# Mamba-2 scan with a quick-GELU layer on one core: second group's first two blocks by seven block products, w_in's sums in four portions, four buffers for x

## The chip, the core and the metric

The kernel runs on one core of a Trainium2 chip. A core has a matrix engine (TensorE, "PE" in the profile, with its weight loads as "PEld"), a vector engine (VectorE, "DVE"), a scalar engine (ScalarE, "ACT"), GpSimd ("POOL") and the engine that issues most of the transfers here (SyncE, "SP"). Each works through its own list of instructions in order, and waits on semaphores that other engines and transfers raise. The metric is the device time of one execution in microseconds (us); of several runs the median is given.

## The reference

A chunked state-space scan gives 3072 tokens of 256 channels, and a two-layer network with a quick-GELU follows. Cut to what matters:

```python
# x (4, 8, 768, 32), a (4, 8, 768), B and C (4, 8, 768, 16)
for c in range(nc):                                   # chunks of 32
    cum = np.cumsum(log_a[:, :, sl], axis=-1)
    L = np.exp(cum[:, :, :, None] - cum[:, :, None, :]) * causal
    y[:, :, sl] = einsum('bhij,bhjd->bhid', (Cc @ Bc^T) * L, xc) \
                  + einsum('bhin,bhnd->bhid', Cc, state) * np.exp(cum)[..., None]
    state = decay_full * state + sum_j(Bc_j xc_j decay_from_j)
x = y.transpose(0, 2, 1, 3).reshape(3072, 256)
h = x @ w_in                                          # (256, 2048), float64 weights
out = (h * sigmoid(1.702 * h)) @ w_out                # (2048, 256)
```

The weights come as 64-bit floats, and the kernel makes 32-bit ones of them on VectorE and ScalarE in the first 70 us.

## The kernel before

**Tiling.** The 3072 tokens are six groups (g = 0 to 5) of TG = 512. A group has two "pairs" of 128-token chunks, numbered p or k = 2g and 2g+1. For a group the scan's result is yT[g] (256 channels by 512 tokens, as two halves of channels and two of tokens). The 2048 hidden rows are 16 tiles of 128, taken two at a time as eight blocks j = 0 to 7; gT[g, j] holds a block's activations.

**The scan of a pair.** `decay(p)` is one long VectorE scan (L402, into L) and two small products (`ends`, Be, L461). `gain` makes 56 small matmuls into the banks A (L711); `part_of` masks A into the state S, on ScalarE (L762) or VectorE (L764); `add_up` chains the states (L777); `since_start` makes CsT (L665). `turn_blocks` transposes B and C on VectorE (L635); `mask_blocks` makes CT on ScalarE (L657); `score` makes 64 small matmuls into cb (L680); `weigh` multiplies L by cb on VectorE (L691). `finish` step 0 ("inter") makes y from the old state (L816), step 1 ("intra") from L and x (L828), and ScalarE copies y into yT (L855). cb, y and the sums acc of w_out's products share one area of PSUM, so each waits for the readers of the one before.

**A block as whole products or as seven block products.** `hidden(g, f)` makes one hidden tile by two products of 512 columns (L884) and one ScalarE silu (L888). `first(g, j, i)` makes a block (two hidden tiles) by seven products of 128 by 128 by 256 instead of eight, in the Strassen-Winograd manner. It needs sums of w_in (`mix_in(n)`: four VectorE instructions for blocks 2n and 2n+1) and of yT (`mix_y(g)`, three instructions, L908 to L910). In the lists of steps "j.i" is product i of block j: 1, 6, 7, 4 add up in a bank X, and between them ScalarE copies the partial sum out (L945: after 1 and 7 into ac, after 6 into b), which the next product of X waits for; after 4 it takes the silu of X (L917). 5, 2, 3 go into a bank Y. D is the VectorE sum of Y and ac (L1072, 512 columns), S its silu; after 3 comes the VectorE sum of Y and b (L1072, 256 columns), T is its silu. X, Y and A take turns on four PSUM banks ("ff"), so a new X or Y waits for the last reader of an older one. `product(g, j, i)` are the seven products with w_out ("P", L1045, and L1052 in the last group); they need `mix_w` (sums of w_out, L1005) and `mix_g(g, j)` (sums of gT, L908 to L910).

**Order around the change.** The order on each engine is the order of the code (`in_order` at the end fixes it). Group 0 is done by whole products: 16 `hidden`, then `project_all` (w_out, L982), with the second pair's conversion and scan work hung in between by `at(in_project[0], i, ...)`. Then group 1 begins: blocks 0 and 1 by `hidden(1, f)`, f = 0 to 3, with group 2's scan work after the first two and the output of group 0 (`turn_out`, two VectorE transposes, L1099, and eight output transfers) after the others; then blocks 2 to 7 by seven products:

```python
at(after, "H0", lambda: decay(n + 1), lambda: mix_y(1), lambda: since_start(n),
   lambda: since_start(n + 1), lambda: gain(later), lambda: keep_both(later, True), lambda: score(later),
   lambda: weigh(n), lambda: weigh(n + 1))
at(after, "H1", lambda: turn_out(0, 0), lambda: turn_out(0, 1))
...
run(1, "2.1 3.1 2.5 2.6 3.6 z 2.2 2.7 3.5 3.7 3.2 2.D 2.4 3.D 3.4 2.S W 2.3 3.S 3.3 2.T 3.T y",
    z=lambda: finish(later, (0,)), y=lambda: finish(later, (1,)), W=lambda: mix_w(0))
for j in range(2):
    mix_g(1, j)
run(1, "4.1 4.5 4.2 P P 4.6 P L P 4.7 P P P 4.D", seven(1, 0), L=more_loads)
```

From group 2 on every block is done by seven products, and `mix_in(0)`, for blocks 0 and 1, is made at the end of group 1. Some products in group 1 are issued in two or four parts of the columns (n in `hidden` and in `product`).

**Transfers.** All of SP's transfers are in one list. `load(p)` brings the pair's b and x (and from group 2 on the blocks zC and zB); `spread(p)` brings the decay factors a; each x tile has three buffers, so x of pair 5 takes the buffer of pair 2 and waits for its last reader.

Of the kernel before, what the change touches and what calls it, by code (L numbers as in the profile page):

```python
# [8 lines left out]
FP32 = mybir.dt.float32  # L9
# [7 lines left out]
P = 128  # L17
# [18 lines left out]
def kernel(  # L36
# [31 lines left out]
    nc = tc.nc  # L68
# [69 lines left out]
    def load(p, parts=None):  # L138
# [4 lines left out]
        for part in parts:  # L143
            dst, src, e = {"b": (rb, B, N), "c": (rc, C, N), "x": (rx, x, D)}[part]
            dst[p] = raw.tile([P, 2, NH, e], FP32, tag=part, name=f"{part}{p}",
                              bufs=2 if part == "c" else 3)
            for k in range(2):
                b, c = divmod(2 * p + k, NC)
                sl = slice(c * P, (c + 1) * P)
                nc.sync.dma_start(out=dst[p][:, k], in_=src[b, :, sl, :].rearrange("h s d -> s h d"))  # L150
# [567 lines left out]

    steps = const.tile([P, Q * D, 2 * CG], FP32, name="steps")
    drop = ffn.tile([P, 4, TG // 2], FP32, tag="my", name="drop", bufs=1)[:, :2].rearrange(  # L720
# [171 lines left out]

    def mix_in(n):

# [5 lines left out]
        for o, u, v, op in ((s1, a21, a22, ALU.add), (s2, s1, a11, ALU.subtract),  # L900
                            (s3, a11, a21, ALU.subtract), (s4, a12, s2, ALU.subtract)):
            nc.vector.tensor_tensor(out=o, in0=u, in1=v, op=op)
        for k in range(2):
# [112 lines left out]
    def product(g, j, only=ORDER, ks=range(2)):  # L1016
# [22 lines left out]
        for i in only:  # L1039
            w, h = terms[i]  # L1040
            if g < NG - 1:
                n = 2 if g == 1 and 7 * j + ORDER.index(i) < 0 else 1
                for k in range(n):
# [181 lines left out]
    for i, k, c in ((2, 1, 1), (3, 2, 2), (4, 4, 4), (5, 6, 8), (6, 9, 12), (7, 12, 15)):  # L1225
# [12 lines left out]
       lambda: weigh(PG), lambda: weigh(PG + 1))  # L1238
    at(in_project[0], 13, lambda: finish(pairs, (0,)))
    at(in_project[0], 15, lambda: finish(pairs, (1,)))  # L1240
    at(in_project[0], 13, lambda: mix_in(1), lambda: mix_in(2), lambda: mix_in(3),
       lambda: turn_blocks(2), lambda: decay(n))
    at(in_project[0], 6, lambda: spread(n), lambda: load(n), lambda: load_blocks(n + 1),
# [3 lines left out]

    after = {}

    later = n, n + 1  # L1250
    at(after, "H0", lambda: decay(n + 1), lambda: mix_y(1), lambda: since_start(n),
       lambda: since_start(n + 1), lambda: gain(later), lambda: keep_both(later, True), lambda: score(later),
       lambda: weigh(n), lambda: weigh(n + 1))
    at(after, "H1", lambda: turn_out(0, 0), lambda: turn_out(0, 1))
    assert [b for b in range(NB) if 3 * CG <= b * NC < 4 * CG] == [2]
# [6 lines left out]
    project_all(0, in_project[0])  # L1262
    mask_blocks(n)
    mask_blocks(n + 1)
    load(p)
    spread_rows(2)
    for step in "H0", "H1":
        for i in range(2):
            hidden(1, 2 * int(step[1:]) + i)
        for do in after[step]:  # L1270
            do()

    def run(g, steps, products=(), **do):
# [36 lines left out]
    def more_loads():  # L1310
# [3 lines left out]

    run(1, "2.1 3.1 2.5 2.6 3.6 z 2.2 2.7 3.5 3.7 3.2 2.D 2.4 3.D 3.4 2.S W 2.3 3.S 3.3 2.T 3.T y",
        z=lambda: finish(later, (0,)), y=lambda: finish(later, (1,)), W=lambda: mix_w(0))
    for j in range(2):
        mix_g(1, j)
    run(1, "4.1 4.5 4.2 P P 4.6 P L P 4.7 P P P 4.D", seven(1, 0), L=more_loads)
    mix_w(1)  # L1320
# [10 lines left out]
    mix_g(1, 6)  # L1331
    mix_in(0)
    run(1, "P P A P P P P P", seven(1, 5), A=lambda: ahead(2, p))
    mix_g(1, 7)

    for g in range(2, NG):
# [44 lines left out]
        else:  # L1381
            run(g, "2.1 1.S 1.4 1.3 2.6 2.5 2.2 2.7 1.T 2.D M0 3.1 3.5 2.S 2.4 3.6 2.3 3.2 3.7 2.T 3.D M1",
                M0=lambda: mix_g(g, 0), M1=lambda: mix_g(g, 1))
# [56 lines left out]
```

## Time and profile before

| | us |
|---|---|
| median of 3 runs | 352.09 (350.5 to 352.2) |
| the profiled execution | 350.75 |
| its span, first to last instruction | 348.7 |
| TensorE busy | 342.2 (98%) |
| VectorE busy | 254.4 (73%) |
| ScalarE busy | 151.7 (44%) |

The granted TensorE clock is 1.000. The page's slices show how the engines are filled over the span; each digit is the busy share of 8.7 us in tenths:

```profile
PE   8989999999999999999999999999999999999996
...
DVE  5989998899679998739996548788454654455463
ACT  5598683106454323744342544432554321554320
```

Group 1 begins in the tenth slice (81.65 us). A row of the timeline gives the start, the length, the engine, the line, the operation, the tiles, the shapes and the number of instructions merged in it; in brackets stands how long the engine had been idle and what ended that. One product of 256 columns shows as two matmul records; the records overlap, so a product's pitch is shorter than its two lengths together. "SPq" rows are transfers being issued, not moved.

### The profile page before, as it was taken

The page shows a single profiled execution, that of the slowest core. Times are in us where ns is not written, and L with a number is a line of the kernel's source. Part 1 is how long each engine was busy: PE and PEld are TensorE (multiplying, and loading weights), DVE is VectorE, ACT ScalarE, POOL GpSimd, SP SyncE. Part 2 cuts the span into 40 slices and gives each one's busy share as a digit, 9 for nine tenths or more (in the row PEclk, how much of TensorE's full clock was granted, in tenths as well). Part 3 has the DMA queues.
Part 4 walks back from the last instruction along what each step waited for, and adds up shares of the span by engine and source line. Part 5 has one row for each costly group of instructions (what it writes and reads, how often), then busy time and mean ns, then how long its engine had stood idle before and what let it go on. Part 6 is the DMA issues. An engine that isn't in the chain of part 4 may idle for free.

```text
span 348.7 us, 8126 instructions
## 1 busy us (share of the span) xinstructions
PE 342.2 (98%) x3386; PEld 273.8 (79%) x3386; DVE 254.4 (73%) x476; ACT 151.7 (44%) x348; POOL 13.8 (4%) x42
## 2 busy tenths in 40 slices
PE   8989999999999999999999999999999999999996
PEld 6634444548888888888888888888888888899996
DVE  5989998899679998739996548788454654455463
ACT  5598683106454323744342544432554321554320
POOL 8400000100000100000000000000000000000000
PEclk9999999999999999999999999999999999999999
DMA  6599988453626100445703026400000300000301
GB/s 160 114 352 192 242 180 222 80 92 69 118 46 138 46 0 9 70 88 107 112 22 55 2 75 112 74 0 3 0 4 2 61 2 0 0 2 0 62 0 61
DMA packets 89980, 25.92 MB, mean 74 GB/s; under 512 B 73432, under 2 KB 87128, under 8 KB 89944
## 3 DMA queue, kind: packets, MB, share of 16 engines
q1 hardware_dynamic: 89112, 24.88, 33.5%
q10 hardware_dynamic: 832, 0.52, 0.6%
q8 instruction: 26, 0.43, 0.5%
q14 instruction: 10, 0.08, 0.1%
HBM read 22.15 MB, written 3.24 MB: 73 GB/s over the span
## 4 chain that ended last, share of the span: by engine, by line
PE 95%; DVE 2%; DMA 2%; SPq 0%; ACT 0%; issue 0%; DVEq 0%
PE acc L1045 28%; PE X L940 19%; PE Y L950 14%; PE h L884 9%; PE o L982 8%; PE acc L1052 7%; PE y L828 2%; PE cb L680 2%; DMA bits<-in_moe_w_in_dram 2%; PE y L816 1%; PE A L711 1%; PE busy L440 1%; PE ab L554 1%; SPq L180 0%; DVE c L1076 0%; PE ab L548 0%
## 5 line engine op out<-in xcount | busy, mean ns | idle before, releaser
L945 ACT ACTIVATE ac<-X 128x256 f32<-128x256 f32 x76 | 29.1, 383 | 78.7 <-PE X L940 78.2
L1045 PE MATMUL acc<-mg,mw 128*128 128x256 f32 x192 | 54.5, 379 | 0.0
L917 ACT ACTIVATE gT<-gT 128x512 f32<-128x512 f32 (+1 forms) x76 | 39.3, 520 | 33.5 <-DVE gT L1072 32.8
L1072 DVE TENSOR_TENSOR gT<-Y,ac 128x512 f32<-128x512 f32 x38 | 26.2, 689 | 36.5 <-PE Y L950 29.9
L940 PE MATMUL X<-my,mi 128*128 128x256 f32 x152 | 45.1, 379 | 0.0
L1072 DVE TENSOR_TENSOR gT<-Y,b 128x256 f32<-128x256 f32 x38 | 15.8, 419 | 34.4 <-PE Y L950 34.4
L1045 PEld LDWEIGHTS acc<-mg,mw 128*128 128x128 f32 x192 | 36.5, 190 | 5.0
L884 PE MATMUL h<-yT,w_in 128*128 128x512 f32 (+2 forms) x108 | 35.7, 486 | 1.4 <-DVE w_in L228 1.4
L1045 PE MATMUL acc<-gT,w_out 128*128 128x256 f32 x128 | 35.5, 379 | 0.0
L884 PEld LDWEIGHTS h<-yT,w_in 128*128 128x128 f32 x108 | 18.3, 190 | 17.3 <-issue 14.9
L940 PEld LDWEIGHTS X<-my,mi 128*128 128x128 f32 x152 | 28.0, 190 | 3.7
L982 PE MATMUL o<-gT,w_out 128*128 128x512 f32 x64 | 28.6, 597 | 0.0
L908 DVE TENSOR_TENSOR mg<-gT 128x512 f32<-128x512 f32 x40 | 27.2, 681 | 0.0
L1045 PEld LDWEIGHTS acc<-gT,w_out 128*128 128x128 f32 x128 | 24.2, 190 | 3.4 <-ACT yT L855 0.2
L945 ACT ACTIVATE b<-X 128x256 f32<-128x256 f32 x38 | 14.6, 384 | 20.2 <-PE X L940 19.8
L940 PE MATMUL X<-yT,w_in 128*128 128x256 f32 x76 | 23.2, 389 | 0.0
L950 PE MATMUL Y<-my,mi 128*128 128x256 f32 x76 | 22.7, 381 | 0.1
L950 PE MATMUL Y<-yT,w_in 128*128 128x256 f32 x76 | 22.7, 381 | 0.0
L940 PE MATMUL X<-my,w_in 128*128 128x256 f32 x76 | 22.5, 379 | 0.0
L950 PE MATMUL Y<-yT,mi 128*128 128x256 f32 x76 | 22.5, 379 | 0.0
L982 PEld LDWEIGHTS o<-gT,w_out 128*128 128x128 f32 x64 | 11.8, 190 | 13.2 <-issue 12.7
L402 DVE TENSOR_TENSOR_SCAN L<-a,idents 128x1024 f32<-128x1024 f32 x9 | 20.5, 2277 | 0.1
(152 smaller groups left out, 545.3 us busy)
## 6 DMA issues: line engine op xcount, KB each, us to landing
a<-scratch SPq DMA_DIRECT2D x18, 256.0 KB, 5.4
bits<-in_moe_w_out_dram SPq DMA_DIRECT2D x8, 512.0 KB, 5.8
x<-in_x_dram SPq DMA_DIRECT2D x24, 128.0 KB, 3.1
out_dram<-ob SPq DMA_DIRECT2D x40, 64.0 KB, 1.9
bits<-in_moe_w_in_dram SPq DMA_DIRECT2D x8, 256.0 KB, 5.1
bits<-in_moe_w_in_dram SPq DMA_DIRECT2D x4, 512.0 KB, 9.7
b<-in_B_dram SPq DMA_DIRECT2D x20, 64.0 KB, 2.9
af<-in_a_dram SPq DMA_DIRECT2D x3, 384.0 KB
```

Source lines behind the costliest of these rows:

```text
L402: nc.vector.tensor_tensor_scan(out=L, data0=ra[p].rearrange("p k e -> p (k e)"), data1=idents.rearrange("p h i -> p (h i)"), initial=0.0, ...
L680: nc.tensor.matmul(out=s["cb"][side, r, k].rearrange("p (q i) -> p q i", q=Q), lhsT=BT[rows, k, side], rhs=CT[rows, k, :, side], start=Tru ...
L884: nc.tensor.matmul(out=h[:, cols], lhsT=w_in[:, f, k], rhs=yT[g][:, k, cols], start=(k == 0 and e == 0), stop=(k == NK - 1), skip_group_ch ...
L908: nc.vector.tensor_tensor(out=t[:, 0:2], in0=B[:, :, 1], in1=B[:, 0], op=ALU.subtract)
L917: nc.scalar.activation(o, i, AF.Silu, scale=GELU_SCALE)
L940: nc.tensor.matmul(out=s["X"], lhsT=lhsT, rhs=rhs, start=i == "1", stop=i == "4", skip_group_check=True)
L945: nc.scalar.activation(copy, s["X"], AF.Copy)
L950: nc.tensor.matmul(out=o, lhsT=lhsT, rhs=rhs, start=s.pop("new", False), stop=i != "5", skip_group_check=True)
L982: nc.tensor.matmul(out=o[c], lhsT=w_out[:, c, f], rhs=gT[g, f // 2][:, f % 2], start=(f == 0), stop=(f == NF - 1), skip_group_check=True)
L1045: nc.tensor.matmul(out=acc[g][0][i][:, cols], lhsT=w, rhs=h[:, cols], start=(j == 0 and k == 0 and (i, 0) in begins), stop=(j == NF // 2 - ...
L1052: nc.tensor.matmul(out=o[k] if type(o) is list else o[:, cols], lhsT=h[:, cols], rhs=w, start=(j == 0 and (i, k) in begins), stop=(j == NF ...
L1072: nc.vector.tensor_tensor(out=o, in0=v, in1=w, op=ALU.add)
```

## The change

Six edits. (1) Blocks 0 and 1 of group 1 are made by seven block products each, in the list of steps, instead of by `hidden`; group 2's scan work is placed among them (G: `gain` and VectorE's `part_of`, C: `score`, t: `since_start`, A and B: `add_up`, w: `weigh`); ScalarE's part of `keep_both` for these pairs becomes VectorE's. (2) `mix_in(0)` moves from the end of group 1 to the projection of group 0; `mix_in(1)` to m, after 0.D; `mix_in(2)` and `mix_in(3)` to V and U, before 2.D. (3) `turn_blocks(2)`, `mask_blocks` of both pairs and `decay(n)` move ahead in the projection of group 0. (4) x has four buffers, and `steps` takes a turn of the "ob" tiles. (5) `turn_out(0, ...)` moves behind the first products with w_out (o). (6) The first eight products with w_out in group 1 are issued in halves of their columns, and in the last group 2.4 stands ahead of 3.5. The parameter `engine` of `mix_in` isn't used by any call.

```diff
--- before.py
+++ after.py
@@ -143,7 +143,7 @@
         for part in parts:
             dst, src, e = {"b": (rb, B, N), "c": (rc, C, N), "x": (rx, x, D)}[part]
             dst[p] = raw.tile([P, 2, NH, e], FP32, tag=part, name=f"{part}{p}",
-                              bufs=2 if part == "c" else 3)
+                              bufs={"c": 2, "b": 3, "x": 4}[part])
             for k in range(2):
                 b, c = divmod(2 * p + k, NC)
                 sl = slice(c * P, (c + 1) * P)
@@ -716,7 +716,8 @@
                             skip_group_check=True)
             increment[p] = [t[:, 2 * n:2 * n + 2] for t in A] if pairs[0] else A
 
-    steps = const.tile([P, Q * D, 2 * CG], FP32, name="steps")
+    steps = ffn.tile([P, 2, DM], FP32, tag="ob", name="steps").rearrange(
+        "p k (e m) -> p (k e) m", m=2 * CG)
     drop = ffn.tile([P, 4, TG // 2], FP32, tag="my", name="drop", bufs=1)[:, :2].rearrange(
         "p a (e m) -> p (a e) m", m=2 * CG)
     nc.gpsimd.memset(drop[:, :, 0:1], 0.0)
@@ -890,7 +891,7 @@
 
     mixed_in, mixed_y, chain = {}, {}, {}
 
-    def mix_in(n):
+    def mix_in(n, engine=nc.vector):
 
         t = wide.tile([P, PN], FP32, tag=("m", "p2")[n % 2], name=f"mi{n}").rearrange(
             "p (j s e) -> p j s e", j=2, s=4)
@@ -899,7 +900,7 @@
         s1, s2, s3, s4 = (t[:, :, i] for i in range(4))
         for o, u, v, op in ((s1, a21, a22, ALU.add), (s2, s1, a11, ALU.subtract),
                             (s3, a11, a21, ALU.subtract), (s4, a12, s2, ALU.subtract)):
-            nc.vector.tensor_tensor(out=o, in0=u, in1=v, op=op)
+            engine.tensor_tensor(out=o, in0=u, in1=v, op=op)
         for k in range(2):
             mixed_in[2 * n + k] = t[:, k]
 
@@ -1039,7 +1040,7 @@
         for i in only:
             w, h = terms[i]
             if g < NG - 1:
-                n = 2 if g == 1 and 7 * j + ORDER.index(i) < 0 else 1
+                n = 2 if g == 1 and 7 * j + ORDER.index(i) < 8 else 1
                 for k in range(n):
                     cols = slice(k * HT // n, (k + 1) * HT // n)
                     nc.tensor.matmul(out=acc[g][0][i][:, cols], lhsT=w, rhs=h[:, cols],
@@ -1237,21 +1238,15 @@
     at(in_project[0], 9, lambda: score(pairs), lambda: gain(pairs), lambda: keep_both(pairs, True),
        lambda: weigh(PG), lambda: weigh(PG + 1))
     at(in_project[0], 13, lambda: finish(pairs, (0,)))
+    at(in_project[0], 13, lambda: turn_blocks(2), lambda: mask_blocks(n), lambda: mask_blocks(n + 1))
     at(in_project[0], 15, lambda: finish(pairs, (1,)))
-    at(in_project[0], 13, lambda: mix_in(1), lambda: mix_in(2), lambda: mix_in(3),
-       lambda: turn_blocks(2), lambda: decay(n))
+    at(in_project[0], 13, lambda: decay(n), lambda: mix_in(0))
     at(in_project[0], 6, lambda: spread(n), lambda: load(n), lambda: load_blocks(n + 1),
        lambda: load(n + 1, "b"), lambda: spread(n + 1))
     at(in_project[0], 9, lambda: load(n + 1, "x"))
 
 
-    after = {}
-
     later = n, n + 1
-    at(after, "H0", lambda: decay(n + 1), lambda: mix_y(1), lambda: since_start(n),
-       lambda: since_start(n + 1), lambda: gain(later), lambda: keep_both(later, True), lambda: score(later),
-       lambda: weigh(n), lambda: weigh(n + 1))
-    at(after, "H1", lambda: turn_out(0, 0), lambda: turn_out(0, 1))
     assert [b for b in range(NB) if 3 * CG <= b * NC < 4 * CG] == [2]
 
 
@@ -1260,16 +1255,8 @@
         for do in in_hidden[0].get(f, []):
             do()
     project_all(0, in_project[0])
-    mask_blocks(n)
-    mask_blocks(n + 1)
     load(p)
     spread_rows(2)
-    for step in "H0", "H1":
-        for i in range(2):
-            hidden(1, 2 * int(step[1:]) + i)
-        for do in after[step]:
-            do()
-
     def run(g, steps, products=(), **do):
 
 
@@ -1312,11 +1299,25 @@
         load(p + 1)
         spread(p + 1)
 
-    run(1, "2.1 3.1 2.5 2.6 3.6 z 2.2 2.7 3.5 3.7 3.2 2.D 2.4 3.D 3.4 2.S W 2.3 3.S 3.3 2.T 3.T y",
-        z=lambda: finish(later, (0,)), y=lambda: finish(later, (1,)), W=lambda: mix_w(0))
+    def keep_later():
+        gain(later)
+        for k in later:
+            part_of(k, range(4), False)
+
+    def add_later(i):
+        add_up(later[i], range(4))
+
+    decay(n + 1)
+    mix_y(1)
+    run(1, "0.1 0.2 G 0.5 0.6 C t A 0.7 1.1 1.2 0.D m 0.4 1.6 B 1.5 0.3 0.S 1.7 2.1 0.T 1.D w 1.4",
+        G=keep_later, A=lambda: add_later(0), B=lambda: add_later(1), C=lambda: score(later), t=lambda: [since_start(k) for k in later], m=lambda: mix_in(1), w=lambda: (weigh(n), weigh(n + 1)))
+    run(1, "1.S 3.1 1.3 1.T 2.5 2.6 3.6 2.2 z 2.7 3.5 3.7 3.2 V U 2.D 2.4 3.D 3.4 2.S W 2.3 3.S 3.3 y 2.T 3.T",
+        z=lambda: finish(later, (0,)), y=lambda: finish(later, (1,)), W=lambda: mix_w(0), m=lambda: mix_in(1), V=lambda: mix_in(2), U=lambda: mix_in(3),
+        w=lambda: (weigh(n), weigh(n + 1)))
     for j in range(2):
         mix_g(1, j)
-    run(1, "4.1 4.5 4.2 P P 4.6 P L P 4.7 P P P 4.D", seven(1, 0), L=more_loads)
+    run(1, "4.1 4.5 4.2 P P 4.6 P L P 4.7 P o P P 4.D", seven(1, 0), L=more_loads,
+        o=lambda: (turn_out(0, 0), turn_out(0, 1)), U=lambda: mix_in(3))
     mix_w(1)
     mix_g(1, 2)
     decay(p)
@@ -1329,7 +1330,6 @@
     k = NF // 2 - 1
     run(1, closing(k), seven(1, 4))
     mix_g(1, 6)
-    mix_in(0)
     run(1, "P P A P P P P P", seven(1, 5), A=lambda: ahead(2, p))
     mix_g(1, 7)
 
@@ -1379,7 +1379,7 @@
             if most:
                 decay(p)
         else:
-            run(g, "2.1 1.S 1.4 1.3 2.6 2.5 2.2 2.7 1.T 2.D M0 3.1 3.5 2.S 2.4 3.6 2.3 3.2 3.7 2.T 3.D M1",
+            run(g, "2.1 1.S 1.4 1.3 2.6 2.5 2.2 2.7 1.T 2.D M0 3.1 2.4 2.S 3.5 3.6 2.3 3.2 3.7 2.T 3.D M1",
                 M0=lambda: mix_g(g, 0), M1=lambda: mix_g(g, 1))
         for j in range(5 if more else 4, NF // 2):
             if j == 5:
```

## The prediction

> **What bounds the kernel now.** First the page: TensorE is busy for nearly the whole span, and the chain that ended last is TensorE for 95%.
>
> ```profile
> PE 342.2 (98%) x3386; PEld 273.8 (79%) x3386; DVE 254.4 (73%) x476; ACT 151.7 (44%) x348; POOL 13.8 (4%) x42
> PE 95%; DVE 2%; DMA 2%; SPq 0%; ACT 0%; issue 0%; DVEq 0%
> ```
>
> Then the view of waits for TensorE: it lists no wait behind 22 us. The view of windows for the changed stretch, 81.65 (first hidden product of group 1) to 99.62 (product 4.1), says the same: TensorE 17.97 of 17.97 us, VectorE 14.17.
>
> ```profile
> PE h L884 <- DVE w_in L228: 1.4, 1, 1.4
> 81.65:99.62 17.97, 17.97 (x385) 15.44 (x383) 14.17 (x30) 10.60 (x29) 0.00 (x0) 1.00 0.49 93
> ```
>
> So a gain has to be TensorE work taken away, and what VectorE and ScalarE make late comes back as TensorE waits. The timeline of the stretch has the rows I price with (start us, length us):
>
> ```profile
> 70.70 2.35 DVE L691 TENSOR_TENSOR L<-L,cb 128x1024 f32<-128x1024 f32 x2
> ...
> 77.36 1.09 DVE L635 STREAM_TRANSPOSE Ct<-zC 128x512 f32<-128x512 f32 x1
> ...
> 79.26 2.22 DVE L402 TENSOR_TENSOR_SCAN L<-a,idents 128x1024 f32<-128x1024 f32 x1
> 79.26 1.00 SPq L150 DMA_DIRECT2D x<-in_x_dram  x2
> ...
> 81.65 3.71 PE L884 MATMUL h<-yT,w_in 128*128 128x128 f32 x28
> ...
> 81.92 2.28 DVE L402 TENSOR_TENSOR_SCAN L<-a,idents 128x1024 f32<-128x1024 f32 x1
> ...
> 85.28 0.84 PE L711 MATMUL A<-x,Be 64*32 64x64 f32 x56
> ...
> 86.10 1.20 PE L680 MATMUL cb<-CT,Bt 32*64 32x128 f32 x64
> 86.18 1.70 ACT L762 ACTIVATE S<-A,part 128x64 f32<-128x64 f32 x8 [0.19 <-PE A L711]
> ...
> 87.23 3.72 PE L884 MATMUL h<-yT,w_in 128*128 128x256 f32 x16
> ...
> 90.79 1.03 PE L940 MATMUL X<-yT,w_in 128*128 128x256 f32 x4
> ...
> 91.43 1.30 DVE L1099 STREAM_TRANSPOSE ob<-c 128x512 f32<-128x512 f32 x2
> ...
> 95.71 0.69 DVE L1072 TENSOR_TENSOR gT<-Y,ac 128x512 f32<-128x512 f32 x1 [2.98 <-ACT ac L945]
> ```
>
> VectorE runs without a break from 62 to 92.73, and then has 2.98 us to spare, and 0.26 more before the next sum. That 3.2 us is the cover the change draws on.
>
> **TensorE work, waits left out.** Two blocks of hidden rows cost 81.65 to 85.28 (3.63) and 87.23 to 90.79 (3.56), 7.19 us. Seven products each make 14 of two records; the chain gives 0.86 us for four such records, so 0.432 a product. A change to or from the small tiles costs 0.09 going in (85.19 to 85.28) and 0.10 coming out (the first record after cb takes 0.32 against 0.216). A and cb, side by side before, now stand apart, so one more pair of these. In the place of 7.19: two products 0.86, in 0.09, (A as before), out 0.10 and two products 0.86, in 0.09, (cb as before), out 0.10 and ten products 4.32: 6.42. **Saved: 0.77 us.** The new split of the first eight w_out products in halves of 128 columns costs 0.447 (hidden's quarters: 4 x 0.1117) against 0.432, eight times 0.015: **+0.12**.
>
> **VectorE, step by step.** Added ahead of 4.1: mix_in(0), 1.465 (twelve mix_in instructions take 72.96 to 77.36); four sums L1073, two D and two "3", 2 x 0.61 + 2 x 0.335 at their pitch (95.71's row is 0.69 long; the next starts 0.08 before its end); part_of, which ScalarE did, 0.80 (four L764 in group 2: 131.36 to 132.16). Taken away: turn_out, 1.30. Net 2.85 against 3.2 of cover. Put in the new order, next-free times in us:
> - weigh of k=2,3 ends 73.05 as before; both transposes 1.90 (77.36 to 79.26): 74.86. Their blocks landed by 71.97. decay(4) with its two Be 2.66: 77.52; mix_in(0): 78.99.
> - decay(5) takes the L buffer that the intra products of k=2 read until 79.1 (half of the 128 records from 78.38): starts 79.2, 2.73 with Be: 81.95. Its a landed at 77.88.
> - mix_y(1) 1.52: 83.47, which was 86.17. part_of needs A, on TensorE from 82.60, done 0.90 later as at 85.28: 83.50, then 84.30. CsT 0.67: 84.97. add_up of k=4 1.3: 86.2.
> - 0.D needs the second ac copy: 86.77 (below), a 0.57 wait that absorbs part_of. Free 87.38; mix_in(1) 88.84; add_up of k=5 0.9: 89.75; sum 0.3 ends 90.17; 1.D ends 90.78; weigh ends 93.05; sum 1.3 ends 93.38; mix_in(2) and (3) free at 96.23; 2.D ends 96.92, 3.D 97.53; mix_w(0), two sums: mix_g starts at 99.58. It was 99.40.
>
> **TensorE with waits.** A product's copy on ScalarE begins 0.63 after the product, lasts 0.38, and TensorE follows some 0.06 later (VectorE to TensorE 0.055: 305.015 to 305.07). So a product may follow the one whose copy it needs after 1.08 us; two products between give 1.30, one gives 0.86.
> - 0.1 81.65; A 82.60 (Be5 82.0, c copies end 82.44: just in time); 0.5 83.39; 0.6 83.93; cb 84.45; 0.7 85.61. Its copy ends 86.73, which is 0.D's wait. 1.1 86.15, 1.2, 0.4, 1.6, 1.5, 0.3 88.30, 1.7 88.74, 2.1 89.17.
> - 1.4 is wanted at 89.60, with one product between: 89.82. Wait 0.22 and 0.10 for the restart: **0.32**.
> - 3.1 90.36; it needs Y0's bank, free 90.22. 1.3 needs 1.D's sum, 90.84: **0.15**. 2.5 91.37, 2.6, 3.6, 2.2, inter 93.19; it takes cb's area, so weigh must have ended: 93.10, just.
> - 2.7 94.28 needs the copy of 2.6. In ScalarE's queue that stands behind silu 1.T, which waits for sum 1.3: 93.38 + 0.42 + 0.38 = 94.2, just in time. 3.5, 3.7, 3.2, 2.4, 3.4 follow; 2.3 at 96.97 meets 2.D's end by 0.00; 3.3 wanted at 97.41 waits for 3.D: 97.585, **0.28** with restart. Intra 98.21, 4.1 **99.62**.
>
> The waits sum to 0.75, and the saving to 0.77: 4.1 starts where it did. After it VectorE is 0.18 late, but mix_g(0) (ends 101.1) is wanted by a product after 102.3, and the 1.30 of turn_out falls into the 1.74 that VectorE idles before 104.27. The last mix_in(0), 1.465, leaves group 1's end, where TensorE waits for nothing: 0.
>
> **The edits that cost nothing.** mask_blocks' four copies (1.70) move to ScalarE's idle 11.4 us before 79.93. The fourth x buffer lets x5 go at 73.1 in place of 79.26; it landed at 83.43, and A's second half is now wanted at 83.0: without it 0.4 to 0.5 us would be lost. Behind it on SP: the next zC/zB now go when the transposes free them, from 74.4, not 80.37; then x6 waits until 79.26 for its buffer, as x5 did; the a for it is held to 102.5 as before; eight output DMAs (92.17 to 97.18) go after the next loads, near 112, and their tile is not wanted for 50 us. steps in an "ob" tile: its readers end long before the tile's next turn. TensorE's instruction count stays at 3386 records: 16 added by the w_out halves, 16 fewer by the quarters and halves.
>
> **Group 5.** 3.5 at 305.07 waited 0.31 (start to start 0.52 for 0.216). 2.4 now goes first, at 304.77, but needs the copy that ends at 304.92: 304.98, and 3.6 comes at 305.94 where it came at 306.04: **-0.10**.
>
> ```profile
> 304.53 0.38 ACT L945 ACTIVATE ac<-X 128x256 f32<-128x256 f32 x1 [0.91 <-PE X L940]
> ...
> 305.07 0.70 PE L950 MATMUL Y<-my,mi 128*128 128x256 f32 x2
> ```
>
> [...] part_of reads PSUM; ScalarE's eight took 1.70, VectorE's four 0.80. [...]
>
> **Sum.** -0.77 + 0.75 + 0.12 - 0.10 = 0.00: 350.75 of the profiled execution (348.7 span, 2.05 around it) stays 350.75. The runs' median, 352.09, is 1.34 above that execution; I carry it: **352.1**.
>
> **Rivals.**
> - *The waits don't come* (0.23). Two of the three hang on 0.2 us or less of VectorE; were its pitches a little shorter, 0.43 of the 0.75 goes, and with 1.4 all of it: -0.4 to -0.75, **351.5**. For: VectorE waits 0.57 at 0.D, so it starts the tail afresh. Against: from 86.77 it has not one free moment.
> - *VectorE becomes the bound* (0.15), slower. From 0.D to 3.D its queue is solid, and each 0.1 us more there is 0.1 at 3.3. Rows with an extra wait start 0.07 later than those without (add_up: 0.10 against 0.035); some eleven of the new waits could have it: 0.8, **352.9**. It decides once the lateness is over 0.1. Against: before shows most waits taken up beneath the instruction ahead.
> - *The buffer doesn't free the load* (0.07): SP held elsewhere, x5 lands at 83.4, A is 0.5 late and all after it: **352.6**.
> - *Forecast* 0.55: 351.7 to 352.5.
>
> Range: the runs spread over 1.7 us, and medians can fall on either end, so 352.1 - 0.75 - 1.2 = 350.1 to 352.1 + 0.8 + 0.2 = 353.1. About 0.5% (1.76 us) is what can be told from no change; one case alone hardly reaches it, a low median with the first rival could: faster 0.20, same 0.72, slower 0.08.
>
> **What would show it.** 4.1 within 0.3 of 99.62; gaps on TensorE before 1.4, 1.3 and 3.3; VectorE solid from 86.8 to 102; A unbroken. Wrong if TensorE has no gaps there (first rival), or if 2.7 waits for ScalarE by 0.3 or more (second).

## The result, and the profile after

| us | before | after |
|---|---|---|
| median of 20 runs each | 351.87 (350.35 to 352.91) | 351.79 (350.37 to 354.26) |
| the profiled execution | 350.75 | 350.55 |
| its span | 348.7 | 348.8 |
| 0.1, first product of group 1 | 81.65 | 81.40 |
| 0.1 to 4.1 | 17.97 | 18.05 |
| 4.1 to the last group's first w_out product | 208.57 | 208.87 |
| from there to TensorE's last record | 37.42 | 37.42 |

The ratio after to before is 1.0005, 95% interval 0.9989 to 1.0021: no difference that can be measured. 352.1 was predicted, on the median of three runs of before, which lies 0.2 above the one of these 20. Line numbers from about L720 on are one higher than before.

The page of the changed kernel, its first lines, and the two waits of TensorE behind 10 us that its view of waits lists beside two at the start:

```profile
span 348.8 us, 8132 instructions
...
PE 342.9 (98%) x3386; PEld 273.0 (78%) x3386; DVE 257.4 (74%) x484; ACT 152.1 (44%) x348; POOL 14.0 (4%) x42
```

```profile
PE h L885 <- DVE w_in L228: 0.6, 1, 0.6
PE y L829 <- issue: 0.6, 1, 0.6
```

The wait for w_in was 1.4 before. It ended at 22.51 here and at 22.76 there, and group 1 begins 0.25 earlier for it, in a part of the program that the change doesn't touch. From 81.65 to 99.62, as before shown, the windows say (span, then busy time of TensorE, its weight loads, VectorE, ScalarE, GpSimd):

```profile
81.65:99.62 17.97, 17.89 (x369) 13.72 (x368) 17.53 (x46) 9.09 (x24) 0.00 (x0) 1.00 0.29 57
```

VectorE went from 14.17 to 17.53 of 17.97 us: its cover is used up. TensorE's 385 records became 369, and yet the stretch is as long as it was. TensorE's timeline shows why:

```profile
81.40 0.59 PE L941 MATMUL X<-yT,w_in 128*128 128x256 f32 x2
...
82.36 0.87 PE L711 MATMUL A<-x,Be 64*32 64x64 f32 x56
83.27 0.70 PE L951 MATMUL Y<-my,mi 128*128 128x256 f32 x2
83.82 0.67 PE L941 MATMUL X<-my,mi 128*128 128x256 f32 x2
...
89.11 0.59 PE L941 MATMUL X<-yT,w_in 128*128 128x256 f32 x2
89.75 0.70 PE L941 MATMUL X<-my,w_in 128*128 128x256 f32 x2
90.28 0.59 PE L941 MATMUL X<-yT,w_in 128*128 128x256 f32 x2
90.72 0.67 PE L951 MATMUL Y<-yT,mi 128*128 128x256 f32 x2
...
95.96 1.03 PE L941 MATMUL X<-my,w_in 128*128 128x256 f32 x4
96.82 1.28 PE L951 MATMUL Y<-yT,mi 128*128 128x256 f32 x4
98.03 1.48 PE L829 MATMUL y<-L,x 64*32 64x64 f32 x128
99.45 0.70 PE L941 MATMUL X<-yT,w_in 128*128 128x256 f32 x2
```

A product that waits for nothing starts 0.43 after the one before it. 1.4 (89.75) starts 0.64 after 2.1, and its own first record lasts 0.10 longer (0.70 for 0.59): 0.31 lost. A row of 0.67 for a pair (1.3, at 90.72) has a gap of 0.07 inside it, and the row of four at 96.82 (2.3 and 3.3) is 1.28 long where four take 1.03: 0.25. These are the three predicted waits, the third spread over 2.3 and 3.3. A fourth one, not predicted, lies before 0.5 (83.27): it comes 1.87 after 0.1, where other executions of the same order show as little as 1.73 (e3, e4 and e10 below), so 0.14. A fifth lies in the row of 0.6 (83.82), 0.67 long as that of 1.3: 0.07. e3, e4 and e10 don't have it either. The view of waits names none of the five: all are too short for its list, and are found only by the starts and lengths of neighbouring rows.

VectorE's timeline in the same stretch:

```profile
79.79 2.29 DVE L402 TENSOR_TENSOR_SCAN L<-a,idents 128x1024 f32<-128x1024 f32 x1 [0.50 <-DMA a<-scratch]
...
85.76 0.93 DVE L778 SCALAR_TENSOR_TENSOR S<-S,since 128x64 f32<-128x64 f32 x3
86.71 0.69 DVE L1073 TENSOR_TENSOR gT<-Y,ac 128x512 f32<-128x512 f32 x1
...
96.07 1.28 DVE L1073 TENSOR_TENSOR gT<-Y,ac 128x512 f32<-128x512 f32 x2
...
99.40 0.68 DVE L909 TENSOR_TENSOR mg<-gT 128x512 f32<-128x512 f32 x1
```

decay(5) was due at 79.2 and waited 0.50 for its a, which SP issued at 72.96, 1.1 later than in the execution before; mix_y(1) behind it is what 0.5 and 0.6 wait for. At 0.D (86.71 for 86.77 predicted) VectorE was to wait 0.57. Here it comes straight from `add_up` (85.76 + 0.93), so the lateness has used up that wait; in e3 and e10, where decay(5) doesn't wait for a, 0.58 of idle time stands there. The pair 2.D and 3.D ends at 97.35, mix_g starts at 99.40.

Behind 4.1 the changed kernel's execution has a wait that the one before had not. All engines' timeline (PEld is TensorE's weight load):

```profile
108.28 2.29 DVE L402 TENSOR_TENSOR_SCAN L<-a,idents 128x1024 f32<-128x1024 f32 x1 [0.49 <-DMA a<-scratch]
...
117.70 0.40 DVE L1073 TENSOR_TENSOR gT<-Y,b 128x256 f32<-128x256 f32 x1
...
118.46 0.36 ACT L946 ACTIVATE ac<-X 128x256 f32<-128x256 f32 x1
...
118.88 0.30 PEld L941 LDWEIGHTS X<-my,mi 128*128 128x128 f32 x2 [0.45 <-ACT ac L946]
```

Read from the top: VectorE waits 0.49 for pair 6's a; up to the sum "3" at 117.70 it idles only once more, 0.54 before 116.03, for GpSimd, which works there on what VectorE has just made, so the lateness is handed on; the silu of that sum holds ScalarE until 118.46; the copy behind it is what a product waits for, 0.21 and 0.10 for the restart: 0.31. In group 5, product 3.1 starts at 304.56 and 2.3 at 306.59, 2.03 apart, where they were 2.14 apart (304.33 and 306.47).

So the profiled executions differ by -0.25 (start), +0.07 (group 1's stretch) and +0.30 (+0.12 halves, -0.10 group 5, +0.31 the new wait, -0.03 unassigned): +0.12, the 0.1 of the spans.

### The profile page after: what moved, and what is told of

Read it like the earlier page. It is cut to its first block, busy times and chain, and to the rows that moved or that the text cites. A ratio compares the mean times of both kernels' runs of the same rounds, so it can differ in the third digit from the quotient of the medians.

```text
span 348.8 us, 8132 instructions
## 1 busy us (share of the span) xinstructions
PE 342.9 (98%) x3386; PEld 273.0 (78%) x3386; DVE 257.4 (74%) x484; ACT 152.1 (44%) x348; POOL 14.0 (4%) x42
## 4 chain that ended last, share of the span: by engine, by line
PE 96%; DMA 1%; DVE 1%; SPq 1%; issue 0%; ACT 0%; DVEq 0%
PE acc L1046 28%; PE X L941 21%; PE Y L951 15%; PE o L983 8%; PE acc L1053 7%; PE h L885 7%; PE y L829 2%; PE cb L680 2%; PE y L817 1%; DMA bits<-in_moe_w_in_dram 1%; PE A L711 1%; PE busy L440 1%; PE ab L554 1%; SPq L180 1%; PE ab L548 0%; DVE L L691 0%
## 5 line engine op out<-in xcount | busy, mean ns | idle before, releaser
L946 ACT ACTIVATE ac<-X 128x256 f32<-128x256 f32 x80 | 30.6, 382 | 79.5 <-PE X L941 79.0
L918 ACT ACTIVATE gT<-gT 128x512 f32<-128x512 f32 (+1 forms) x80 | 41.3, 519 | 35.5 <-DVE gT L1073 34.9
L1046 PE MATMUL acc<-mg,mw 128*128 128x256 f32 (+1 forms) x198 | 54.5, 373 | 0.0
L941 PE MATMUL X<-my,mi 128*128 128x256 f32 x160 | 47.8, 382 | 0.0
L1046 PE MATMUL acc<-gT,w_out 128*128 128x256 f32 (+1 forms) x134 | 35.5, 370 | 0.0
L885 PE MATMUL h<-yT,w_in 128*128 128x512 f32 x64 | 28.2, 596 | 0.6 <-DVE w_in L228 0.6
L941 PE MATMUL X<-yT,w_in 128*128 128x256 f32 x80 | 24.5, 388 | 0.0
L885 PEld LDWEIGHTS h<-yT,w_in 128*128 128x128 f32 x64 | 11.9, 190 | 15.5 <-issue 12.4
L951 PE MATMUL Y<-yT,mi 128*128 128x256 f32 x80 | 24.0, 382 | 0.0
L941 PE MATMUL X<-my,w_in 128*128 128x256 f32 x80 | 23.9, 382 | 0.1
```

The costliest lines, as they stand in the source:

```text
L885: nc.tensor.matmul(out=h[:, cols], lhsT=w_in[:, f, k], rhs=yT[g][:, k, cols], start=(k == 0 and e == 0), stop=(k == NK - 1), skip_group_ch ...
L918: nc.scalar.activation(o, i, AF.Silu, scale=GELU_SCALE)
L941: nc.tensor.matmul(out=s["X"], lhsT=lhsT, rhs=rhs, start=i == "1", stop=i == "4", skip_group_check=True)
L946: nc.scalar.activation(copy, s["X"], AF.Copy)
L951: nc.tensor.matmul(out=o, lhsT=lhsT, rhs=rhs, start=s.pop("new", False), stop=i != "5", skip_group_check=True)
L1046: nc.tensor.matmul(out=acc[g][0][i][:, cols], lhsT=w, rhs=h[:, cols], start=(j == 0 and k == 0 and (i, 0) in begins), stop=(j == NF // 2 - ...
```

## The experiments

Theory: the block products save TensorE 0.7 to 0.8, and the chain of sums and copies, with VectorE full, gives it back as short waits; each wait has its own cause, and should go when that cause is taken away. For a common measure each run's profile gives two lengths: from the last output product of group 0 (one product, 0.43, ahead of 0.1) to 4.1, "the stretch", and from 4.1 to the last group's first w_out product, "the way". Single times differ by 2 us for reasons told below, so the verdicts go by these. All runs but the last are single ones.

| run | time | stretch | way |
|---|---|---|---|
| before | 350.75 | 18.41 | 208.57 |
| after | 350.55 | 18.48 | 208.87 |
| e1_three_x | 350.29 | 18.59 | 208.79 |
| e2_loads_early | 352.48 | 18.33 | 208.55 |
| e3_no_halves | 352.57 | 18.25 | 210.01 |
| e4_parts_scalar | 351.67 | 18.25 | 208.99 |
| e5_swap_alone | 350.75 | 18.39 | 208.67 |
| e9_turn_out_back | 352.19 | 19.51 | 208.83 |
| e11_pads_no_halves | 350.76 | 18.30 | 209.27 |
| e6_pool_sums | 351.04 | 18.02 | 208.56 |
| e10_more_halves | 354.37 | 18.24 | 210.79 |
| e8_all | 348.53 | 18.06 | 208.54 |
| e12_all_timed | 350.10 (median of 12) | 18.62 | 208.58 |

The runs of before beside them had 351.61 (e1 to e4), 350.75 (e5, e8, e9, e11) and a median of 351.21 (e6, e10, e12).

**Three buffers for x.**

```diff
-                              bufs={"c": 2, "b": 3, "x": 4}[part])
+                              bufs={"c": 2, "b": 3, "x": 3}[part])
```

> The changed kernel with three x buffers again. Theory (the fourth buffer only takes the x load of pair 5 out of the way, worth 0.4 to 0.5 us): SP again waits until about 79.3 with that load, it lands near 83.4, and the second half of A and product 0.5 start 0.3 to 0.6 us later than in the changed kernel; the stretch from product 0.1 to 4.1 is 18.3 to 18.6 us instead of 18.05. Rival (the load was hidden anyway): the stretch stays at 18.05 within 0.1.

The small products into A came to 1.12 us from their start to 0.5, and 0.5 followed 0.1 by 2.08. In executions with four buffers it followed by 1.73 (e3, e4, e10) to 1.87 (after). So the buffer is worth 0.35 us beside the first of these, 0.21 beside the last; x5 was issued at 78.53 with three, at 74.24 with four (after). From 0.1 to 4.1 it took 18.16 (the table's stretch begins 0.43 earlier): less than the theory's 18.3, and just more than the rival's 18.15. The changed kernel's own 18.05 holds 0.21 of lateness from a, which e1 doesn't have; beside the 17.82 of e3 and e4, e1 is 0.34 longer. SP's list, with three buffers, around it (transfers being issued, three rows in a row):

```profile
69.98 1.24 SPq L256 DMA_DIRECT2D a<-scratch  x2
78.53 1.00 SPq L150 DMA_DIRECT2D x<-in_x_dram  x2
79.63 3.04 SPq L124 DMA_DIRECT2D zC<-in_C_dram  x4
```

SP stands still from 71.2 to 78.5: the wait of one transfer holds all that are behind it.

**The next loads early.** `more_loads` goes ahead of V, seven us sooner.

```diff
-    run(1, "1.S 3.1 ... 3.7 3.2 V U 2.D ...",
+    run(1, "1.S 3.1 ... 3.7 3.2 L V U 2.D ...",
...
-    run(1, "4.1 4.5 4.2 P P 4.6 P L P 4.7 P o P P 4.D", ...
+    run(1, "4.1 4.5 4.2 P P 4.6 P P 4.7 P o P P 4.D", ...
```

> The changed kernel with the loads for pairs 6 and 7 (more_loads) about 8 us earlier. Theory (the product at 118.88 waits because the decay factors of pair 6 land at 108.2, half a us after VectorE is ready for them, and VectorE hands that lateness on through its queue, the silu and the copy): VectorE starts decay(6) without a wait near 107.8, the gap of 0.21 us and its restart of 0.10 at 118.9 are gone, and the time from 4.1 to the product 2.7 of group 5 falls from 204.68 to 204.35 to 204.40 us. Rival (VectorE is late there for its own work, whatever the transfer does): the gap stays.

The way fell by 0.32, to 208.55, the wait at 118.9 was gone, and 2.7 of group 5 came 204.36 after 4.1, as the theory says. VectorE's timeline:

```profile
109.61 2.28 DVE L402 TENSOR_TENSOR_SCAN L<-a,idents 128x1024 f32<-128x1024 f32 x1
...
119.03 0.40 DVE L1073 TENSOR_TENSOR gT<-Y,b 128x256 f32<-128x256 f32 x1
```

The bracket with the wait for the transfer is missing, and the sum "3" comes 17.68 after 4.1 (101.35) in place of 18.25. The single time, 352.48, was longer nevertheless: a wait of 1.8 for w_in at 21 us, and halts at 15 and 80 us of the kind told below.

**No halves.**

```diff
-                n = 2 if g == 1 and 7 * j + ORDER.index(i) < 8 else 1
+                n = 2 if g == 1 and 7 * j + ORDER.index(i) < 0 else 1
```

> The changed kernel without the halves of the first eight w_out products (16 fewer matmul records). Theory (a product in halves costs 0.015 us more, eight of them 0.12): the time from 4.1 to the acc products behind is 0.12 us shorter, all else the same. Rival (the halves keep the number of TensorE records at 3386, and another number moves waits elsewhere): a new gap of more than 0.1 us shows on TensorE somewhere behind, or the total moves by more than 0.3 us in the stages after 100 us.

The rival came: in place of 0.12 less, the way grew by 1.14. TensorE's timeline in the intra products of group 2:

```profile
151.44 0.99 PE L829 MATMUL y<-L,x 64*32 64x64 f32 x74
153.45 0.77 PE L829 MATMUL y<-L,x 64*32 64x64 f32 x54 [1.03 <-issue]
```

"issue" says that the engine waited for nothing that the profile shows. The halt cuts the 128 products of one step behind the 74th.

**No halves, and eight small products more at the very start**, so that the records number 3386 again:

```diff
-                n = 2 if g == 1 and 7 * j + ORDER.index(i) < 8 else 1
+                n = 2 if g == 1 and 7 * j + ORDER.index(i) < 0 else 1
...
-    keep_busy(5, 0)
+    keep_busy(5, 8)
```

> The kernel without halves of the w_out products, which lost 1.24 us among the small matmuls of group 2 (near 152 us), with 16 matmul records added at the very start, where TensorE waits (32 by 32 products of ones), so that the count is 3386 again. Theory (TensorE's instructions come in blocks over the instruction queue, and the loss is a late block that falls among the small matmuls when the count ahead of them is another): no wait by issue near 152 us, and the time from 4.1 to the last group's first w_out record is 208.55 to 208.85 us instead of 210.01. Rival (the halves themselves do it, by what they move in the stage behind): the 1.24 us wait is there again.

The halt was gone. That speaks for the place of the small products in the list of instructions as the cause, and against the lack of halves, from one execution of each. (The way was 209.27 all the same, above the theory's 208.85: in this execution a of pair 6 kept VectorE waiting 0.97, and the product at 118.9 lost 0.61, one at 112.3 another 0.23.)

**Sixteen products in halves**, 16 more records:

```diff
-                n = 2 if g == 1 and 7 * j + ORDER.index(i) < 8 else 1
+                n = 2 if g == 1 and 7 * j + ORDER.index(i) < 16 else 1
```

> The changed kernel with the first 16 products with w_out in halves in place of 8: 16 more records on TensorE, 3402. By the sizes of the trace the eight more halves cost 8 x 0.015 = 0.12 on the way from 4.1 to the last group's first w_out product: 208.99 if the number of records is free. Rival, from the kernel without halves (16 fewer records, 1.24 us of waits among the small intra products of group 2 with nothing to wait for): the blocks of 128 products in which the program comes to TensorE shift by 16 records the other way, and a wait of 0.3 to 1.4 us falls among other small products, or goes; then the way is 209.3 or more, with TensorE idle for no releaser among small products.

Again the rival: 210.79, 1.8 more than the sizes say, and now the halt is in group 4. TensorE's timeline, then the instruction queue on the page:

```profile
259.30 1.45 PE L829 MATMUL y<-L,x 64*32 64x64 f32 x125
262.43 0.30 PE L829 MATMUL y<-L,x 64*32 64x64 f32 x3 [1.67 <-issue]
```

```profile
q8 instruction: 26, 0.43, 0.5%
```

That queue brings 26 pieces of 0.43 MB / 26 = 16.5 KB in every run. The halts of all thirteen profiles (lost time among small products without a releaser), by the number of matmul records ahead of them, fall on five places only:

| behind record | where | seen in | us, start to start |
|---|---|---|---|
| 349 | scan of pairs 0 and 1, 15 us | each of the 13 | 0.18 to 1.15 |
| 854 | group 0's last intra, 78 to 80 us | e2, e3, e4, e6, e9, e10, e11, e12 | 0.33 to 1.71 |
| 1234 | group 1's intra, 99 us | e12 | 0.63 |
| 1744 | group 2's intra, 152 us | e3 | 1.24 |
| 2891 | group 4's intra, 260 us | e10 | 1.89 |

The numbers are those of the list, not of the code: in e11 the code behind its pads comes 16 records later, and its halts stand behind 349 and 854 all the same. The distances 505, 380, 510 and 1147 are 4, 3, 4 and 9 times 126 to 128 records, which with a weight load each make some 255 instructions. A piece of 16.5 KB would give each of them 65 bytes, by these numbers an estimate. The 3386 records make some 26 stretches of 127, as many as the queue has pieces, and these move all through the run: in the changed kernel's profile from 9.5 to 330.6 us, with 114 matmul records begun ahead of the first and 3257 ahead of the last, 126 for each. One to three halts show in a run, of up to 1.89 us. Two of them end at a like distance from a piece: the one behind 349 at 16.08 in the changed kernel, 2.8 after a piece began to move at 13.3, and the one of e10 at 262.43, 2.4 to 2.9 after one that began between 259.5 and 260.0.

How long the 127 records ahead of such a number run says part of the rest:

| up to record | runs | us for 127 records | halt |
|---|---|---|---|
| 1744 | e3 | 1.73 | 1.24 |
| 1744 | after, e4, e11, e12 | 4.43 | none |
| 2891 | e10 | 1.39 | 1.89 |
| 2891 | after, e4, e11, e12 | 3.98 to 3.99 | none |
| 1234 | e12 | 4.55 | 0.63 |
| 1234 | e8_all (the same program) | 4.54 | none |
| 854 | before, after | 5.07, 5.06 | none |
| 854 | e3, e4, e10, e12 | 5.09 | 0.33 to 1.71 |

A piece of small products alone (1.39 and 1.73 us) seems to be run through before the next is there; one with more large products among them (3.98 us and more) often is not, and sixteen records more or fewer change which it is. At 1234 and 854 even 4.5 and 5.1 us are not always enough, and the same program halts in one execution and not in the other; what else decides there was not tried. That the halts come from late pieces of this queue is the author's estimate, from places, sizes and times; the trace doesn't name it.

**part_of on ScalarE.**

```diff
-            part_of(k, range(4), False)
+            part_of(k, range(4), True)
```

> The changed kernel with part_of of pairs 4 and 5 on ScalarE (eight activations) instead of VectorE (four). Theory (it is hidden behind 0.D's wait on either engine; ScalarE's 1.70 us push the copy of 0.6): the stretch from 0.1 to 4.1 is 18.05 within 0.1 us, 0.7 starts up to 0.1 later, and VectorE idles 0.8 us more before 0.D. Rival (the work belongs on ScalarE, VectorE is the bound throughout): the stretch falls by 0.3 us or more.

No difference: the stretch is 18.25 as in e3, which has it on VectorE, with the same waits before 1.4, 1.3, 2.3 and 3.3 to 0.01. VectorE idles 1.33 before 0.D, 0.75 more than in e3; 0.7 starts 3.93 after 0.1 in both, so it isn't later either. From 0.1 to 4.1 it took 17.82, outside the theory's 18.05 within 0.1, but e3 shows that this is not part_of's doing: the wait for a of pair 5 is missing in both.

**turn_out ahead of 2.D again.** 1.30 us of transposes back where VectorE is full; q stands for them, and o goes.

```diff
-    run(1, "1.S 3.1 ... 3.2 V U 2.D ...",
+    run(1, "1.S 3.1 ... 3.2 V U q 2.D ...",
```

> The changed kernel with turn_out's two VectorE transposes (1.30 us) put into VectorE's full queue, just ahead of 2.D. Theory (VectorE is the bound of the stretch: what it gets more there, TensorE waits for at 2.3 and 3.3): product 2.3 starts 1.2 to 1.3 us later against 0.1 than in the changed kernel, and the stretch from the last o record to 4.1 grows from 18.25 to 18.48 to 19.4 to 19.8 us. Rival (there is slack left before 2.3, the waits there are ScalarE's copies): the stretch grows by less than 0.5 us.

VectorE's timeline, then TensorE's:

```profile
96.29 1.30 DVE L1100 STREAM_TRANSPOSE ob<-c 128x512 f32<-128x512 f32 x2
97.51 1.25 DVE L1073 TENSOR_TENSOR gT<-Y,ac 128x512 f32<-128x512 f32 x2
```

```profile
98.22 1.30 PE L951 MATMUL Y<-yT,mi 128*128 128x256 f32 x4 [1.01 <-DVE gT L1073]
```

For 1.22 us more on VectorE (96.29 to 97.51) the gaps at 2.3 and 3.3, restart included, grew from 0.26 to 1.44: nearly one for one. The stretch, 19.51, lies in the theory's range. Product 2.3 starts 1.02 later against 0.1 than in the changed kernel, not 1.2 to 1.3: 0.5 and 0.6 didn't wait for a here. Against e3 and e4, where they didn't either, it is 1.24. From about 93 to 97 VectorE sets the end; there is no cover left.

**w_in's sums for blocks 4 to 7 on GpSimd.**

```diff
-        V=lambda: mix_in(2), U=lambda: mix_in(3),
+        V=lambda: mix_in(2, nc.gpsimd), U=lambda: mix_in(3, nc.gpsimd),
```

> The changed kernel, with the sums of w_in for blocks 4 to 7 (mix_in(2), mix_in(3)) on GpSimd, 2.93 us off VectorE ahead of 2.D. Theory (VectorE's queue sets the last waits): 2.D and 3.D end over 2 us earlier, the gaps at 2.3 and 3.3 (0.09 and 0.17 in the changed kernel's profile) are gone, the one before 1.3 (0.07) stays as it lies ahead of these sums; stretch from group 0's last output product to 4.1 between 18.1 and 18.3. Rival: GpSimd takes so long for the eight sums, or slows VectorE so much while it runs, that 4.1 and what follows wait: stretch, or the way from 4.1 to the last group's first w_out product, longer by 0.3 or more than 18.48 and 208.87.

The waits before 2.3 and 3.3 were gone, those before 1.4 (0.31) and 1.3 (0.07) stayed, the stretch fell to 18.02, a little below the theory's 18.1. GpSimd needs 0.73 for a sum that VectorE makes in 0.42, but has the time, from 67.25 to 73.0. What it cost lies elsewhere. GpSimd's first sum, and VectorE's additions to the state and its products by cb beside these sums:

```profile
67.25 0.72 POOL L903 TENSOR_TENSOR mi<-w_in 128x256 f32<-128x256 f32 x1 [5.96 <-DVE w_out L228]
```

```profile
67.48 3.43 DVE L778 SCALAR_TENSOR_TENSOR S<-S,since 128x64 f32<-128x64 f32 x5
70.83 2.34 DVE L691 TENSOR_TENSOR L<-L,cb 128x1024 f32<-128x1024 f32 x2
```

The five additions take 3.43 in place of 1.44 in the changed kernel; the products by cb, whose second input lies in PSUM, take 1.21 each as ever, though GpSimd's sums go on to 73.0. TensorE's inter, at 73.32, waited 0.65 for the products by cb that come behind these additions, where the changed kernel has no such wait: more than the 0.26 that e6 saves at 2.3 and 3.3.

**The swap in group 5 alone, in the kernel before.**

```diff
-            run(g, "... M0 3.1 3.5 2.S 2.4 3.6 ...",
+            run(g, "... M0 3.1 2.4 2.S 3.5 3.6 ...",
```

> The kernel before with only the order of 2.4 and 3.5 in group 5 changed. Theory: the wait before 3.5 (0.31 us with its restart) is gone and one of 0.21 before 2.4 comes in its place, for the copy of 2.7 into ac; the time from 4.1 to the first L1052 record is 0.10 us less than the 208.57 of the kernel before. Rival (nothing else is late there): 0.31 less.

The wait there fell by 0.10, from 0.31 to 0.21 (the restart of 0.10 comes on top in both). But the way grew by 0.10: at 118.8 the product lost 0.12 and 0.10 in a program that has nothing else of the change. That wait belongs to the old place of the loads, not to the new order alone: of the ten profiles with the loads there, eight have it (0.18 to 0.61), only before and e6 have not; of the three with early loads none has.

**All repairs in one.** More_loads early; the sums mix_in(3) and one of the two turn_outs change places; 3.1 and 2.6 step between the products that wait, and 3.6 and 1.T go further back; B goes behind 0.3; and SP issues the a of decay(5) ahead of the b:

```diff
-    at(in_project[0], 6, ..., lambda: load(n + 1, "b"), lambda: spread(n + 1))
+    at(in_project[0], 6, ..., lambda: spread(n + 1), lambda: load(n + 1, "b"))
...
-    run(1, "0.1 ... 0.D m 0.4 1.6 B 1.5 0.3 0.S 1.7 2.1 0.T 1.D w 1.4",
+    run(1, "0.1 ... 0.D m 0.4 1.6 1.5 0.3 B 0.S 1.7 2.1 0.T 1.D w 3.1 1.4 2.6",
-    run(1, "1.S 3.1 1.3 1.T 2.5 2.6 3.6 2.2 z 2.7 3.5 3.7 3.2 V U 2.D ...",
+    run(1, "1.S 1.3 2.5 2.2 2.7 3.6 1.T z 3.5 3.7 3.2 L V q 2.D ...",
...
-    run(1, "4.1 4.5 4.2 P P 4.6 P L P 4.7 P o P P 4.D", ...
+    run(1, "4.1 4.5 4.2 P P 4.6 P P 4.7 P U o P P 4.D", ...
```

Here q is turn_out(0, 0) and o turn_out(0, 1).

> The changed kernel with four repairs: 3.1 and 2.6 around 1.4 and 1.3 and the sum of 0.3 ahead of add_up of pair 5 (for the wait before 1.4), one of turn_out's transposes in the place of mix_in(3) ahead of 2.D (for the waits before 2.3 and 3.3), the loads of pairs 6 and 7 about 8 us earlier (for the wait at 118.9), and the decay factors of pair 5 loaded ahead of its b (for the wait of 0.5). Theory (these four waits are what eats the saving): the stretch from the last o record to 4.1 is 17.6 to 17.9 us instead of 18.25 to 18.48, and the time from 4.1 to the last group's first w_out record 208.45 to 208.60 instead of 208.87; together 0.8 to 1.0 us less than the changed kernel. Rival (VectorE's total is the bound, and a wait removed comes back behind it): the sum of the two falls by less than 0.4 us.

Stretch 18.06 and way 208.54: together 0.75 less than after, a little under the theory's 0.8, and 0.38 less than before. The way is as the theory says, the stretch 0.16 above its range. The waits before 2.3 and 3.3 are gone, 0.06 is left before 1.3, and the wait before 1.4 has only moved. All engines' timeline:

```profile
89.10 0.38 ACT L946 ACTIVATE ac<-X 128x256 f32<-128x256 f32 x1 [0.34 <-DVE gT L1073]
...
89.38 0.38 ACT L918 ACTIVATE gT<-X 128x256 f32<-128x256 f32 x1
...
89.81 0.30 PEld L951 LDWEIGHTS Y<-my,mi 128*128 128x128 f32 x2 [0.45 <-ACT gT L918]
```

Product 1.4 starts without a wait now. But the copy of 3.1 (89.10) stands ahead of 1.4's silu (89.38) on ScalarE, and waits for a sum of VectorE; 2.5 (89.81) waits for that silu: 0.21 and 0.10 for the restart, nearly 0.32 for the 0.31 that went. In this one place the rival was right. So of the 0.75, about 0.3 is the wait at 118.9, about 0.2 the lateness from a of pair 5, which no run but the changed kernel's has, and about 0.26 the work taken off VectorE ahead of 2.D; exchanging the products brought nothing.

The time, 348.53, was 2.2 below the run of before beside it, which these two lengths don't explain: group 1 also began sooner (0.1 at 79.82), without a wait for w_in. To tell the program from this one execution, it was timed:

> The kernel of e8_all again, now timed. In its one profile the stretch from group 0's last output product to 4.1 took 18.06 us and the way from 4.1 to the last group's first w_out product 208.54, together 0.75 less than in the changed kernel's profile. If that is the program and not that one execution, the median should lie 0.6 to 1.1 us under both kernels, a ratio of 0.9968 to 0.9983 to the one before. Rival: the single 348.53 owed its 2.2 us mostly to a start-up and intra products that happened to run without waits, and the repairs are within the spread: then the median lies within 0.4 us of before (ratio 0.9988 to 1.0012).

350.10 (349.54 to 351.38) against 351.21 (350.16 to 353.4): a ratio of 0.9963, interval 0.9941 to 0.9985. It beats the kernel before, by 0.15 to 0.59%, and lies below the changed kernel's interval too, which was measured against other runs of before. The gain, 1.1 us, is a little more than the theory's ratio of 0.9968 allows, and the two lengths explain 0.4 of it; where the rest comes from isn't shown. Its profiled execution had a stretch of 18.62, which looks like a miss; the view of waits tells why:

```profile
PE y L829 <- issue: 1.3, 2, 0.9
```

One of the two halts behind this line cut group 1's intra at 99.28, 0.63 from start to start where neighbours are 0.02 apart: without it the stretch is 18.01, beside e8_all's 18.06.

## Why the prediction was right

**The sum was right, and for the reason given**: the saving is real and is spent in waits of 0.1 to 0.3, at the places named. Term by term:

- *TensorE work saved*, 0.77: 18.05 less the six gaps (0.14, 0.07, 0.31, 0.07, 0.09, 0.17) is 17.20 against 17.97, so 0.77. e3, without the first two, says the same: 17.82 less 0.64 is 17.18.
- *The wait before 1.4*, 0.32: 0.31. It comes from the product, copy, product chain with only one product in between, and no run that kept that order was without it; the order without it (e8) has one of 0.32 before 2.5 instead.
- *Before 1.3*, 0.15: 0.07. *Before 2.3 and 3.3*, 0.28 in all: 0.26. The second is VectorE's, as e6 (gone with 2.93 us less) and e9 (1.18 longer with 1.22 more) show from two sides. The first stands in e6 too, ahead of the sums that were moved there; its weight load at 90.68 follows VectorE's 1.D, which ends at 90.63.
- *Not foreseen: before 0.5 and 0.6*, 0.21. The prediction took a's landing from the execution before; SP came to it 1.1 later in this one. In no other profile with the change did decay(5) wait for a, so the term is one of the execution; e3, e4 and e10 took 17.81 to 17.82 from 0.1 to 4.1, 0.15 less than before.
- *Halves*, +0.12, and *group 5*, -0.10: the second as predicted twice, in after and in e5. The first is in after's trace; e3's way, less its halt of 1.24, is 208.77, 0.10 below after, and its wait at 118.9 is 0.04 longer, so 0.14.
- *The fourth buffer*, 0.4 to 0.5: 0.35 at most, by e1.
- *"After 4.1 nothing" failed* for the profiled execution: 0.31 at 118.4. The step looked at mix_g and at VectorE's idle time, not at the landing of pair 6's a. But e5 shows that the old order can meet the same wait. How often it does, two profiles of that order can't tell.
- *Record count "at no cost"*: the prediction counted 3386 on both sides, and no new halt came in the changed kernel's profile. Sixteen fewer or more brought halts of 1.24 and 1.89, in one execution each.

Two readings of the prediction were off without bearing on the sum. VectorE's unbroken run in the kernel before begins at 63.19, not at 62. And the 0.57 of idle time before 0.D, which the first rival leaned on, was missing in the changed kernel's profile; in the ten other profiles with the change it is there, 0.58 long and in e4 1.33.

Of the rivals, the buffer's fell (x5 went 4.3 earlier), and "the waits don't come" fell with the three waits. The slower rival, VectorE as the bound, fell too. Its mechanism is real, as e9 shows, but the extra waits it feared in VectorE's queue didn't come: from the start of 0.D to the end of 3.D VectorE took 10.64, in this profile as in e3, and 10.76 was foreseen. It also asked for a wait of 2.7 for ScalarE, and there is none. The 0.07 by which 3.D came late against 0.1 (97.35 - 81.40 = 15.95, 15.88 foreseen) is from a: in e3 it is 15.72.

That the median fell within 0.3 of the forecast is no proof of the sum. The runs of one kernel spread over 2.6 to 3.9 us, and the base of 352.09, from three runs, was 0.2 too high. The lengths inside the trace carry the account, and in the profiled execution two unforeseen waits for a (0.21 and 0.31) were offset by a start 0.25 earlier and by the waits that came out 0.11 smaller.

What stays open: whether the changed program meets the halt at record 854 more often than the one before. The two profiles of the program before (one with the swap) show none, and eight of eleven of the changed one and its variants do; the medians say that it doesn't matter, or that something else pays for it.

## What to carry to other kernels

When TensorE is full and work is taken from it, ask of every product in the new order what it waits for, to a tenth of a microsecond: three gaps of 0.1 to 0.3, too short for any list of waits, ate most of a saving of 0.8. Taking work off the engine that was late, and issuing a load sooner, brought back part of it; changing the order of the products only moved a wait to the next one. Compare lengths between two marks inside the trace rather than whole times, since one execution differs from the next by 2 us in places that the change doesn't touch. And before adding or removing a few instructions, look at where that shifts the dense runs of small matmuls.

## What the runs showed of the hardware

- TensorE halted for 0.2 to 1.9 us from start to start behind fixed numbers of records (349, 854, 1234, 1744, 2891), 126 to 128 or a multiple apart, among small matmuls, in some executions and not in others; with 16 records more or fewer halts came in new places (e3, e10).
- The spread of the runs, some 2 us, has visible places: the end of the wait for w_in (21.6 to 23.6 us, none in e8), the halt at 854 (0 to 1.7), and the landing of a (0 to 0.8 of lost time).
- Beside GpSimd's sums (0.73 each) five of VectorE's small additions took 3.43 in place of 1.44; the two products with one input in PSUM stayed at 1.21 each (e6).
- A gap ahead of a product, be it 0.06 or 1.17, is followed by a first record of 0.32 in place of 0.216; a gap between the two records of one product (0.07 before the second of 1.3) is not.
